# Last parts of experts in quarter blocks: 35 blocks instead of 36, with another order of the first batch's groups

## The chip, the cores and the metric

The kernel runs on one core of one Trainium2 chip. The metric is the device time of one execution in microseconds (us); the median of three runs before the change is 202.54 us (202.13 to 202.78). TensorE multiplies matrices; a weight load (the stationary operand) comes ahead of each matmul and is shown as an engine row of its own, PEld. VectorE (DVE), ScalarE (ACT) and GpSimd (POOL) work elementwise, and SyncE (SP) issues most of the DMA transfers.

## The reference, cut to what matters

Attention with a polynomial sketch feeds a mixture of experts that sends every token to one expert. All of it is in float32.

```python
# q, k, v: (4, 4, 1088, 32); S1, S2: (8, 32)
phi = lambda x: outer(S1 @ x, S2 @ x).reshape(64)        # per row
kv, z = sum_s phi(k) v^T, sum_s phi(k)
x = (phi(q) @ kv) / (phi(q) . z + 1e-6)                  # to (4352, 128)
logits = normalize(x) @ normalize(expert_emb).T / tau    # 8 experts
expert_idx = argmax(logits); gate_w = softmax(logits)[expert_idx]
for e in range(8):
    mask = expert_idx == e
    out[mask] = gate_w[mask, None] * (relu(x[mask] @ w1[e]) @ w2[e])   # F = 1024
```

With the inputs of the reference the eight experts get 524, 552, 568, 587, 623, 527, 504 and 467 of the 4352 tokens.

## The kernel before, in words

The four batches are handled as two pairs (m = 0 and 1). A pair has 17 tiles of 128 rows, in groups of four tiles and a rest of one (`GROUPS`). For a group of the first pair the steps are: turn the keys (`ktr0`, four transposes into a PSUM tile of tag `t`, then a copy by ScalarE), turn the queries (`qtr0`), the key sketch (`kab0`: 8 matmuls into the one PSUM bank `ab`), a copy of its second factor (`kb0`, ScalarE), the key products (`kp0`, VectorE, which reads the bank `ab` and that copy), the query sketch with its repeats (`pairs`: 16 matmuls into both PSUM tiles of tag `big`), two copies out of it (`sec`, ScalarE), two products (`prod`, VectorE), and the sum of keys by values (`kv0`: 16 matmuls for a group of four tiles). A float32 matmul shows as two records in the profile, one for each of its passes.

The program is emitted in an order written out by hand, and every engine keeps it. `HEAD` (L367) is the order of the first pair's steps and `ORDER` (L373) that of what follows; later work is put at a tick and a rank by `put_at`. Each tick is one block of tokens from tick `FIRST` on.

The tokens are grouped by expert into blocks of 128 rows, which are fetched with indirect DMAs (`fetch`), turned (`turn`, L936), multiplied by the first layer (`up`, L974), passed through ReLU (L992), multiplied by the second layer (`down`, L1014) and scattered to the output (L1032). `N` is 4352, and `FULL` is 30 blocks that certainly belong to one expert. The first ten (`EARLY`) are planned from the first pair alone, in `plan_early`; the other ones in `plan_late` (steps `count`, `rest`, `shared`, `others`, `experts`), whose numbers come out of the counts by small VectorE operations, and `table`, which finds the tokens of each block.

What an expert has left over beside whole blocks of 128 goes in halves of 64: the four blocks 30 to 33 (`SHARED`) take two experts, 64 rows each. In such a block (`two(i)`) each of the eight column groups of `up` is four matmuls of 64 stationary columns and 64 moving rows: two experts by two halves of the columns. `down` does two matmuls of 64 stationary columns for each of the eight parts of the sum, one per expert, into the two halves of the output's partitions:

```python
            for b, w in enumerate(ws):
                nc.tensor.matmul(ps[b * HALF:(b + 1) * HALF], h[:, f * P + b * HALF:f * P + (b + 1) * HALF], w[:, f],
                                 start=f == 0, stop=f == NF - 1, skip_group_check=True)
```

The second expert's first layer is loaded to its own place by SP (`weights_b`), and its second layer copied there by ScalarE (`second_weights_b`, L971). The straight line of the program has `USUAL` = 36 blocks. Behind it stands a conditional part for blocks 36 and 37 (`NBLK` = 38), which runs when the number of late blocks, read from memory by each engine (L1139), is above `USUAL - EARLY`.

Of the kernel before, what the change touches and what calls it, by code (L numbers as in the profile page):

```python
# [11 lines left out]
F32 = mybir.dt.float32  # L12
# [21 lines left out]
NBLK = ((N + E * (HALF - 1)) // HALF + 1) // 2  # L34
# [17 lines left out]
LATE = NBLK - EARLY  # L52
SHARED = E // 2
PAIRS = FULL - EARLY
AHEAD = 4
USUAL = N // P + 2
# [9 lines left out]
def kernel(  # L66
# [131 lines left out]
    def word(name):  # L198
        return consts.tile([2 * R, D], U32, name=name)
    top, rem, w, fits = word("s_top"), word("s_rem"), word("s_w"), word("s_fits")  # L200
# [10 lines left out]
    srow = consts.tile([2 * R, D], F32, name="srow")  # L211
# [3 lines left out]
    srows = consts.tile([2 * R, H, D], F32, name="srows")  # L215
# [30 lines left out]
    before, ones = consts.tile([P, P], BF16, name="before"), consts.tile([P, P], BF16, name="ones")  # L246
    less, more = consts.tile([P, E], BF16, name="less"), consts.tile([P, E], BF16, name="more")
    near = consts.tile([P, E], BF16, name="near")
    down_half = consts.tile([HALF, P], BF16, name="down_half")
    base = consts.tile([P, E], BF16, name="base")  # L250
# [9 lines left out]

    nowhere = [consts.tile([P, 2, n], BF16, name=f"nowhere{n}") for n in (EARLY, LATE + SHARED)]

    def more_constants():
        nc.vector.memset(ones, 1.0 / P)
        nc.vector.memset(ones_e, 1.0)

        nc.vector.memset(less, -(P - 1) / (2.0 * P))
        nc.vector.memset(more, (P - 1) / (2.0 * P))

        nc.vector.memset(near, -1.0 / (2.0 * P))  # L270
        nc.vector.memset(c_early, 0.0)
        nc.vector.memset(w_late, float(KEYS * E))
        for t in (place_k, place_r):
            nc.vector.memset(t, -1.0)
        for t, n in zip(nowhere, (EARLY, LATE)):
            nc.vector.memset(t, 0.0)
            nc.vector.memset(t[:, 0, :n], float(NOWHERE))

    def iotas():
# [5 lines left out]
        nc.vector.tensor_scalar(down_half, lane[:HALF], part[:HALF, 0:1], float(HALF), op0=ALU.subtract, op1=ALU.is_equal)  # L285
        nc.vector.tensor_scalar_mul(lanes, bview(lane, [[1, P], [0, WIDE]]), 1.0 / P)
# [69 lines left out]
prod 0 1; kab0 1; kb0 1; pairs 1; kp0 1; sec 1 0; sec 1 1; ktr0 2; qtr0 2; prod 1 0; prod 1 1; kab0 2; kb0 2; pairs 2;  # L356
kp0 2; sec 2 0; sec 2 1; ktr0 3; qtr0 3; prod 2 0; prod 2 1; clear 0; kv0 0; kab0 3; kb0 3; pairs 3; kp0 3; sec 3 0;
sec 3 1; ktr0 r; qtr0 r; prod 3 0; prod 3 1; kv0 1; norm emb; kab0 r; kb0 r; qab0 r; qb0 r; kp0 r; qp0 r; scale emb;
iotas; clear 1; ktr 0; kv0 2; kv0 3; kv0 r
# [84 lines left out]
    def keys(m, c0, c1, tick=None):  # L444
        n = c1 - c0
# [21 lines left out]
        def kv():  # L467

            if c0 == 0:
                acc[m] = ps_one("acc")[:, :8 * D].rearrange("p (i a n) -> p i a n", i=2, a=2)  # L470
            for c in range(c0, c1):
                rest = c == NC - 1
                for i in range(2) if rest else (c // NK,):
                    for p in range(2):
                        for u in range(2):
                            h = 2 * p + u
                            vo = v_rest[m][i][:, h] if rest else v_sb[m][:, h, c]
                            to_ones = (H - h) * D if rest else ((H - h) * 2 * NK - c) * D
                            nc.tensor.matmul(  # L479
                                acc[m][u * HALF:(u + 1) * HALF, i, p], s["kp"][:, c - c0, h],  # L480
                                bass.AP(tensor=vo.tensor, offset=vo.offset,
                                        ap=[list(vo.ap[0]), [to_ones, 2], [1, D]]),
                                start=p == 0 and c == 0, stop=rest, skip_group_check=True)
# [33 lines left out]
        steps.update({f"ktr0 {g}": tr, f"kab0 {g}": ab, f"kb0 {g}": b, f"kp0 {g}": prod, f"kv0 {g}": kv})  # L517
        if c1 == NC:
            steps.update({"total0": total, "trkv0": tr_kv, "kvT0": kvT, "kve0": lambda: kve(0), "kz0": lambda: kve(1)})
# [222 lines left out]
    SIZES = (EARLY, LATE)  # L742
# [3 lines left out]
    exp_i = [consts.tile([1, n], I32, name=f"exp_i{i}") for i, n in enumerate((EARLY, LATE + SHARED))]  # L746

    def blocks(which, upto, weight, place):

        n = SIZES[which]  # L750
        le = work.tile([P, n, E], F32, tag="le", bufs=2, name=f"le{which}")
        at = consts.tile([P, n + which * SHARED], F32, name=f"at{which}")[:, :n]
# [22 lines left out]
    def table(which, m1, key):  # L775
# [3 lines left out]
        n, w = SIZES[which] + which * SHARED, m1 * NCP  # L779
# [5 lines left out]
        def find():  # L785
            shape = [P, 3 * w * n]
            both = consts.tile(shape, BF16, name="hits0") if which == 0 else work.tile(
                [P, NC * ROW * 2], BF16, tag="xg0", bufs=1, name="hits1")[:, :3 * w * n]
# [16 lines left out]
        def first_rows():  # L805
            s["b"] = consts.tile([HALF, 2, SHARED], BF16, name="halves")
            nc.vector.tensor_copy(s["b"], s["ps"].rearrange("p (d n) -> p d n", d=2)[:HALF, :, LATE:])

        def halves():

            ps = s["ps"].rearrange("p (d n) -> p d n", d=2)
            nc.tensor.matmul(ps[:, :, PAIRS:PAIRS + SHARED], down_half, s["b"], start=False, stop=True, skip_group_check=True)

# [6 lines left out]
    def tokens_by_expert(rounded, out, ps):  # L820

        for j, r in enumerate(rounded):
            for i, t in enumerate([r] + counts):
                nc.tensor.matmul(ps[:, j * E:(j + 1) * E], ones, t, start=i == 0, stop=i == len(counts))
        nc.vector.tensor_scalar(out, ps, WHOLE, -WHOLE, op0=ALU.add, op1=ALU.add)

    def plan_early():
# [3 lines left out]
        def count():  # L831
            tokens_by_expert((less,), full, spare[0][:, NC * E:(NC + 1) * E])
# [15 lines left out]
    def plan_late():  # L848
# [4 lines left out]
        full, all_ = both[:, :E], both[:, E:]  # L853
        odd, odds, rank, key = column("odd"), column("odds"), column("odd_rank"), column("odd_key")
# [3 lines left out]
        def count():  # L858
            tokens_by_expert((near, more), both, table_bank[0][:, 1, :2 * E])
# [15 lines left out]
        def shared():  # L875

            s["high"] = column("high", w=SHARED)
            nc.vector.tensor_sub(odd, all_, full)
            nc.vector.tensor_tensor_scan(out=odds[:], data0=ones_e[:], data1=odd[:], initial=0.0, op0=ALU.mult, op1=ALU.add)
            nc.vector.tensor_scalar(rank, odd, -(NO_KEY + 1), NO_KEY, op0=ALU.mult, op1=ALU.add)  # L880
            nc.vector.tensor_add(rank, rank, odds)

            nc.vector.tensor_scalar(pairs, odds[:, E - 1:], 0.5, 0.25, op0=ALU.mult, op1=ALU.add)
            nc.vector.tensor_scalar(pairs, pairs, WHOLE, -WHOLE, op0=ALU.add, op1=ALU.add)
            nc.vector.scalar_tensor_tensor(out=key, in0=full, scalar=-NO_KEY, in1=base, op0=ALU.add, op1=ALU.add)
            n = 2 * SHARED
            is_it = work.tile([P, n, E], F32, tag="emb", bufs=2, name="is_it")
            it = work.tile([P, n, E], F32, tag="emb", bufs=2, name="it")
            s["keys"] = column("odd_keys", w=n)
            nc.vector.tensor_tensor(out=is_it, in0=bview(rank, [[0, n], [1, E]]),  # L890
                                    in1=bview(lane, [[1, n], [0, E]]), op=ALU.is_equal)
            nc.vector.tensor_mul(it, is_it, bview(key, [[0, n], [1, E]]))
            nc.vector.reduce_sum(out=s["keys"][:], in_=it, axis=AX.X)

        def others():
# [5 lines left out]
            halves = s["keys"][:].rearrange("p (n u) -> p n u", u=2)  # L901
            late["second"] = column("second_keys", w=SHARED)[0:1]
            late["keys"] = whole
            nc.vector.tensor_scalar_add(whole[:, LATE:], halves[:, :, 1], NO_KEY)

            nc.vector.tensor_tensor(out=late["second"], in0=whole[0:1, LATE:], in1=last[0:1], op=ALU.min)
            nc.vector.scalar_tensor_tensor(out=last, in0=halves[:, :, 0], scalar=NO_KEY, in1=last, op0=ALU.add, op1=ALU.min)
            late["key"] = whole

        def experts():  # L910
# [5 lines left out]
            nc.vector.tensor_scalar_min(exp_i[1], f, float(E - 1))  # L916
            late["n"] = consts.tile([1, 1], I32, name="n_late")
            nc.vector.tensor_add(late["n"], pairs[0:1], upto[0:1, E - 1:])
        return count, rest, shared, others, experts
# [4 lines left out]
    def of(i):  # L924
        return (0, i) if i < EARLY else (1, i - EARLY)
# [32 lines left out]


# [16 lines left out]
    def up(i):  # L976
# [3 lines left out]
        for u in range(2):  # L980
            for j in range(4):
# [4 lines left out]
                for b, wh in enumerate((w, first_b(i))):  # L986
                    for c in range(2):
                        r = slice(c * HALF, (c + 1) * HALF)
                        nc.tensor.matmul(ps[r, u, j * P + b * HALF:j * P + (b + 1) * HALF],  # L989
                                         wh[:, f * P + c * HALF:f * P + (c + 1) * HALF], x[:, b * HALF:(b + 1) * HALF],  # L990
                                         start=True, stop=True)
# [22 lines left out]
    def down(i):  # L1014
# [3 lines left out]
        for f in range(NF):  # L1018
# [3 lines left out]
            for b, w in enumerate(ws):  # L1022
                nc.tensor.matmul(ps[b * HALF:(b + 1) * HALF], h[:, f * P + b * HALF:f * P + (b + 1) * HALF], w[:, f],  # L1023
                                 start=f == 0, stop=f == NF - 1, skip_group_check=True)
# [54 lines left out]
    count, rest, shared, others, experts = plan_late()  # L1079
# [7 lines left out]
    put(2, 75.5, experts)  # L1087
    put(3, 73.5, find)
# [50 lines left out]
    n_late = nc.values_load(late["n"][:, :], min_val=0, max_val=LATE,  # L1139
                            skip_runtime_bounds_check_because="a count of blocks, of which there are no more")  # L1140
    with tc.If(n_late > USUAL - EARLY):
        put = put_at(-1)
        for i in range(USUAL, NBLK):
            put(0, 0, lambda i=i: fetch(i))
            if i < USUAL + 2:
                put(0, 1, lambda i=i: weights(i))
        put(0, 2, lambda: turn(USUAL))
        in_ticks(USUAL, NBLK, 0)
# [31 lines left out]
```

## Time and profile before

| | |
|---|---|
| median of three runs | 202.54 us |
| profiled execution, its own time | 204.43 us |
| span of the profiled instructions | 202.6 us |
| PE busy | 192.7 us (95%) |
| PE weight loads busy | 182.7 us (90%) |
| ACT, POOL, DVE busy | 102.4, 107.0, 87.6 us |
| granted TensorE clock | full in every slice |
| share of PE in the chain that ended last | 90% |

The span is what the instructions cover; the profiled execution's own time is 1.8 us more. Matmuls are pipelined: a record's duration is the latency of one matmul, and the distance between the starts of two matmuls is what one costs in a stream. In the chain that ended last, a row gives the start, the time until the chain moves on, and the line.

### The profile page before, as it was taken

The numbers are of one execution on the slowest core, as the hardware profiler recorded it, in microseconds if no ns is written. First come the engines' busy times: TensorE is split into PE (matmuls) and PEld (weight loads), VectorE is DVE, ScalarE is ACT, GpSimd is POOL, SyncE is SP. The second block draws the span as 40 slices with busy tenths as digits, with TensorE's granted clock in tenths as the row PEclk, the third lists the DMA queues.
The fourth block names the chain that finished last, engine by engine and source line by source line (L and its number), as shares of the span: only waits on it lengthen the run. The fifth ranks groups of instructions, "written<-read, shape, count | busy, mean of one in ns | idle before, by whom it ended". The sixth has DMA issues, their size and how long they took to land.

```text
span 202.6 us, 6949 instructions
## 1 busy us (share of the span) xinstructions
PE 192.7 (95%) x2586; PEld 182.7 (90%) x2586; DVE 87.6 (43%) x378; ACT 102.4 (51%) x293; POOL 107.0 (53%) x137
## 2 busy tenths in 40 slices
PE   7889999999799999999999999999999999999991
PEld 7667888889689999999999999999999999988991
DVE  6677848888658488912222212222122122112200
ACT  2657451436464456434655546545555465766540
POOL 4000335303813767755878777677676776664043
PEclk9999999999999999999999999999999999999999
DMA  4998799987284886544466665657646784485000
GB/s 132 323 217 287 179 320 293 280 282 208 54 321 139 278 310 211 165 132 145 148 205 189 170 205 155 209 166 163 222 147 184 223 306 169 136 263 190 3 26 25
DMA packets 28162, 39.42 MB, mean 195 GB/s; under 512 B 5738, under 2 KB 21366, under 8 KB 28130
## 3 DMA queue, kind: packets, MB, share of 16 engines
q1 hardware_dynamic: 25776, 34.23, 55.9%
q0 software_dynamic: 2304, 4.74, 7.5%
q8 instruction: 22, 0.36, 0.7%
q14 instruction: 10, 0.08, 0.1%
q10 hardware_dynamic: 50, 0.01, 0.0%
HBM read 34.37 MB, written 4.73 MB: 193 GB/s over the span
## 4 chain that ended last, share of the span: by engine, by line
PE 90%; DVE 4%; ACT 2%; issue 1%; DMA 1%; POOL 0%; POOLq 0%; DVEq 0%
PE ps_big L984 28%; PE ps_ab L1020 14%; PE ps_acc L1020 13%; PE ps_big L613 5%; PE ps_acc L479 4%; PE ps_big L989 4%; PE ps_t L382 3%; PE ps_t L936 2%; PE ps_ab L401 2%; PE ps_big L561 2%; PE ps_acc L1023 2%; PE ps_ab L1023 2%; PE ps_t L802 2%; ACT qpT L570 1%; PE ps_ab L591 1%
## 5 line engine op out<-in xcount | busy, mean ns | idle before, releaser
L984 PE MATMUL ps_big<-xTb,wb 128*128 128x128 f32 x512 | 63.0, 276 | 1.6 <-ACT xTb L938 1.4
L984 PEld LDWEIGHTS ps_big<-xTb,wb 128*128 128x128 f32 x512 | 59.7, 192 | 2.4 <-ACT xTb L938 1.6
L1032 POOL DMA_INDIRECT out_dram<-y,dst_i x36 | 37.7, 1048 | 42.9 <-ACT y L1029 24.4
L992 ACT ACTIVATE hT<-ps_big 128x1024 f32<-128x1024 f32 x36 | 36.9, 1024 | 41.3 <-issue 22.7
L930 POOL DMA_INDIRECT xs<-rows,dst_i x36 | 37.3, 1035 | 18.8 <-DVE dst_i L817 11.3
L938 DVE COPY xTb<-ps_t 128x128 f32<-128x128 f32 x29 | 8.4, 290 | 59.4 <-issue 38.2
L1020 PE MATMUL ps_ab<-w_sb,hT 128*128 x256 | 31.3, 275 | 0.0
L1020 PE MATMUL ps_acc<-w_sb,hT 128*128 x256 | 31.2, 275 | 0.0
L1020 PEld LDWEIGHTS ps_ab<-w_sb,hT 128*128 128x128 f32 x256 | 29.9, 192 | 0.0
L1020 PEld LDWEIGHTS ps_acc<-w_sb,hT 128*128 128x128 f32 x256 | 29.9, 192 | 0.0
L998 POOL TENSOR_TENSOR norm<-norm,half_c 128x1 f32<-128x1 f32 x36 | 21.6, 604 | 4.5 <-ACT sq L997 4.1
L1011 DVE TENSOR_SCALAR gate<-gate 128x1 f32<-128x1 f32 x36 | 5.5, 152 | 23.2 <-ACT probs L1008 16.4
L1029 ACT ACTIVATE y<-ps_ab,gate 128x128 f32<-128x128 f32 x17 | 6.2, 367 | 11.0 <-PE ps_ab L1020 6.4
L1029 ACT ACTIVATE y<-ps_acc,gate 128x128 f32<-128x128 f32 x18 | 6.6, 366 | 9.9 <-PE ps_acc L1020 6.8
L1008 ACT ACTIVATE probs<-xs,norm 128x8 f32<-128x8 f32 x36 | 10.6, 295 | 1.2 <-DVE norm L1001 1.2
L997 ACT ACTIVATE sq<-xs 128x128 f32<-128x128 f32 x36 | 10.8, 301 | 0.2
L936 PE MATMUL ps_t<-ident,xs 128*128 128x128 f32 x36 | 10.2, 282 | 0.2 <-issue 0.2
L417 POOL TENSOR_TENSOR kp<-both 128x1024 f32<-128x1024 f32 (+1 forms) x4 | 6.5, 1624 | 7.0 <-ACT both L412 4.8
L479 PE MATMUL ps_acc<-v,kp 128*64 128x64 f32 x256 | 9.2, 225 | 0.5 <-issue 0.5
L319 POOL TENSOR_TENSOR emb_ss<-emb_ss,half_c 8x1 f32<-8x1 f32 x1 | 0.6, 576 | 17.1 <-ACT emb_sq L318 17.1
L479 PEld LDWEIGHTS ps_acc<-v,kp 128*64 128x64 f32 x256 | 8.2, 138 | 1.5 <-issue 1.5
L989 PE MATMUL ps_big<-xTb,wb 128*64 128x64 f32 x128 | 8.3, 224 | 0.3 <-issue 0.2
(254 smaller groups left out, 293.7 us busy)
## 6 DMA issues: line engine op xcount, KB each, us to landing
wb<-in_moe_w_dram SPq DMA_DIRECT2D x36, 512.0 KB
w_sb<-in_moe_w_dram SPq DMA_DIRECT2D x16, 256.0 KB
rows<-xg SPq DMA_DIRECT2D x4, 544.0 KB
v<-in_v_dram SPq DMA_DIRECT2D x4, 512.0 KB
v<-in_moe_w_dram SPq DMA_DIRECT2D x4, 512.0 KB
k<-in_k_dram SPq DMA_DIRECT2D x3, 512.0 KB
q<-in_q_dram SPq DMA_DIRECT2D x3, 512.0 KB
xs<-rows,dst_i POOLq DMA_INDIRECT x36
```

The lines of the kernel that those rows point to most:

```text
L479: nc.tensor.matmul(acc[m][u * HALF:(u + 1) * HALF, i, p], s["kp"][:, c - c0, h], bass.AP(tensor=vo.tensor, offset=vo.offset, ap=[list(vo.a ...
L930: nc.gpsimd.indirect_dma_start(out=xs[i][:], out_offset=None, in_=rows[:2 * S if t == 0 else N + 1], in_offset=bass.IndirectOffsetOnAxis(a ...
L936: nc.tensor.transpose(ps[:, :P], xs[i][:, :DM], ident)
L984: nc.tensor.matmul(ps[:, u, j * P:(j + 1) * P], w[:, f * P:(f + 1) * P], x, start=True, stop=True)
L989: nc.tensor.matmul(ps[r, u, j * P + b * HALF:j * P + (b + 1) * HALF], wh[:, f * P + c * HALF:f * P + (c + 1) * HALF], x[:, b * HALF:(b + 1 ...
L992: nc.scalar.activation(hT[i], ps, ACT.Relu)
L997: nc.scalar.activation(sq, xs[i][:, :DM], ACT.Square, accum_out=norms[i])
L998: nc.gpsimd.tensor_tensor(out=norms[i], in0=norms[i], in1=half_c, op=ALU.pow)
L1008: nc.scalar.activation(p, xs[i][:, DM:], ACT.Exp, scale=norms.pop(i)[:, 0:1], accum_out=gate[i])
L1020: nc.tensor.matmul(ps, h[:, f * P:(f + 1) * P], ws[0][:, f], start=f == 0, stop=f == NF - 1)
L1029: nc.scalar.activation(y, ps, ACT.Copy, scale=gate.pop(i)[:, 0:1])
L1032: d = nc.gpsimd.indirect_dma_start(out=out[:, :], out_offset=bass.IndirectOffsetOnAxis(ap=dst_i[t][:, j:j + 1], axis=0), in_=y[:], in_offs ...
```

## The change

The leftovers of experts are cut in quarters of 32 rows instead of halves. `near` and `more` get other constants, so that a leftover above 96 rows counts as a whole block and the rest is counted in quarters (`parts`, 1 to 3). Three blocks (30 to 32) take two experts each: 30 and 31 hold a quarter of one and three quarters of another (`MIXED`, `cut(i)` = 32), and 32 holds two halves. The experts are ranked by their number of quarters (`score`, `ahead`, `rank`), and `RANKS` says which rank goes where. What doesn't fit in these six places (`over`) sets off the conditional part, which now has nine blocks and builds a table of its own (`extra`). The straight line has 35 blocks.

In the two mixed blocks a matmul of `up` has 32 or 96 moving rows, and the order of the four matmuls alternates the halves of the columns. `down` does three matmuls per part of the sum there: 32, 32 and 64 stationary columns. In `HEAD` the step `pairs` of groups 1 to 3 stands ahead of `kab0`, `qtr0` ahead of `ktr0`, `kp0` behind the two `prod`, and `kv0 0` is cut in two halves, of which the second comes behind group 3. Nine small memsets and two small VectorE operations are added to the constants (`fours`, `order`, one more pair of `nowhere`; `down_quart`, `last_first`), `halves` of the table becomes two matmuls, and some early tiles move to the pool `work`. In the diff below parts are left out.

```diff
-LATE = NBLK - EARLY
-SHARED = E // 2
+USUAL = N // P + 1
+LATE = USUAL - EARLY
+QUART = P // 4
+SHARED = 3
+MIXED = 2
+RANKS = (4, 5, 2, 0, 1, 3)
+SPILL = 3
+EXTRA = SPILL + E - 2
...
-USUAL = N // P + 2
...
     def more_constants():
         nc.vector.memset(ones, 1.0 / P)
+        nc.vector.memset(fours, 4.0 / P)
...
-        nc.vector.memset(more, (P - 1) / (2.0 * P))
-
-        nc.vector.memset(near, -1.0 / (2.0 * P))
+        nc.vector.memset(more, (QUART - 1) / (2.0 * P))
+
+        nc.vector.memset(near, -(HALF + 1) / (2.0 * P))
+        for i, rank in enumerate(RANKS):
+            nc.vector.memset(order[:, i:i + 1], float(rank))
...
-prod 0 1; kab0 1; kb0 1; pairs 1; kp0 1; sec 1 0; sec 1 1; ktr0 2; qtr0 2; prod 1 0; prod 1 1; kab0 2; kb0 2; pairs 2;
-kp0 2; sec 2 0; sec 2 1; ktr0 3; qtr0 3; prod 2 0; prod 2 1; clear 0; kv0 0; kab0 3; kb0 3; pairs 3; kp0 3; sec 3 0;
-sec 3 1; ktr0 r; qtr0 r; prod 3 0; prod 3 1; kv0 1; norm emb; kab0 r; kb0 r; qab0 r; qb0 r; kp0 r; qp0 r; scale emb;
-iotas; clear 1; ktr 0; kv0 2; kv0 3; kv0 r
+prod 0 1; pairs 1; kab0 1; sec 1 0; sec 1 1; qtr0 2; kb0 1; ktr0 2; prod 1 0; prod 1 1; kp0 1; pairs 2; kab0 2;
+sec 2 0; sec 2 1; qtr0 3; kb0 2; ktr0 3; prod 2 0; prod 2 1; kp0 2; clear 0; kv0 first; pairs 3; kab0 3; sec 3 0;
+sec 3 1; kb0 3; ktr0 r; qtr0 r; prod 3 0; prod 3 1; kp0 3; kv0 second; kv0 1; norm emb; kab0 r; kb0 r; qab0 r; qb0 r;
+kp0 r; qp0 r; scale emb; iotas; clear 1; ktr 0; kv0 2; kv0 3; kv0 r
...
+            nc.vector.scalar_tensor_tensor(out=parts, in0=full, scalar=-4.0, in1=quarters, op0=ALU.mult, op1=ALU.add)
+            nc.vector.tensor_scalar_min(odd, parts, 1.0)
+            score = column("score")
+            nc.vector.scalar_tensor_tensor(out=score, in0=parts, scalar=float(E), in1=last_first, op0=ALU.mult, op1=ALU.add)
...
+    def cut(i):
+        return QUART if i < FULL + MIXED else HALF
...
-                for b, wh in enumerate((w, first_b(i))):
-                    for c in range(2):
-                        r = slice(c * HALF, (c + 1) * HALF)
-                        nc.tensor.matmul(ps[r, u, j * P + b * HALF:j * P + (b + 1) * HALF],
-                                         wh[:, f * P + c * HALF:f * P + (c + 1) * HALF], x[:, b * HALF:(b + 1) * HALF],
-                                         start=True, stop=True)
+                for b, c in ((0, 0), (1, 1), (0, 1), (1, 0)):
+                    r = slice(c * HALF, (c + 1) * HALF)
+                    n0, n1 = ((0, cut(i)), (cut(i), P))[b]
+                    nc.tensor.matmul(ps[r, u, j * P + n0:j * P + n1],
+                                     (w, first_b(i))[b][:, f * P + c * HALF:f * P + (c + 1) * HALF], x[:, n0:n1],
+                                     start=True, stop=True)
...
-            for b, w in enumerate(ws):
-                nc.tensor.matmul(ps[b * HALF:(b + 1) * HALF], h[:, f * P + b * HALF:f * P + (b + 1) * HALF], w[:, f],
-                                 start=f == 0, stop=f == NF - 1, skip_group_check=True)
+            for n0, n1 in ((0, cut(i)), (cut(i), HALF), (HALF, P)):
+                if n0 < n1:
+                    nc.tensor.matmul(ps[n0:n1], h[:, f * P + n0:f * P + n1], ws[int(n0 > 0)][:, f],
+                                     start=f == 0, stop=f == NF - 1, skip_group_check=True)
...
-        for i in range(USUAL, NBLK):
-            put(0, 0, lambda i=i: fetch(i))
+        find, high, low, sums, tokens, *_ = table(2, NM, lambda: late["extra_key"])
+        for f in (extra, find, high, low, sums, lambda: tokens(0, EXTRA)):
+            put_at(-1)(0, -1, f)
+        for i in range(USUAL, USUAL + EXTRA):
+            put_at(max(i - USUAL - AHEAD, -1))(0, 0, lambda i=i: fetch(i))
```

## The prediction

> **What bounds the kernel now.** I read the page first: busy shares, then the chain of work that ended last.
>
> ```profile
> PE 192.7 (95%) x2586; PEld 182.7 (90%) x2586; DVE 87.6 (43%) x378; ACT 102.4 (51%) x293; POOL 107.0 (53%) x137
> ...
> PE 90%; DVE 4%; ACT 2%; issue 1%; DMA 1%; POOL 0%; POOLq 0%; DVEq 0%
> ```
>
> TensorE is the chain for 90% of the span, so a change counts by the PE time that it takes or gives, and by PE's waits in the first 24 us. Next I cut the chain to the shared blocks:
>
> ```profile
> 169.59 0.11 PE ps_t L936
> 169.70 1.79 PE ps_acc L1020 x16
> ...
> 182.93 1.90 PE ps_ab L1023 x32
> 184.83 1.86 PE ps_big L989 x64
> 186.69 0.26 PE ps_t L936
> 186.96 1.90 PE ps_acc L1023 x32
> 188.85 1.98 PE ps_big L984 x16
> ```
>
> An ordinary block is 1.79 (up) + 0.11 (turn) + 1.79 (down) = 3.69 us. The last shared block, from 184.66 to 188.78, is 4.12; the three before it are 4.54, 4.47 and 4.25, two of them with a pause of "issue" inside. The turn takes 0.26 here, not 0.11, though it is the same instruction. The timeline of PE shows why:
>
> ```profile
> 186.41 0.29 PE L989 MATMUL ps_big<-xTb,v 128*64 128x64 f32 x4
> 186.63 0.33 PE L936 MATMUL ps_t<-ident,xs 128*128 128x128 f32 x1
> 186.88 0.32 PE L1023 MATMUL ps_acc<-w_sb,hT 128*64 x1
> 186.89 0.32 PE L1023 MATMUL ps_acc<-v,hT 128*64 128x128 f32 x1
> ```
>
> The four L989 matmuls start in two pairs, at 186.41 and 186.47. A stream of them would go on at 186.53; the turn's weight load begins at 186.62, some 0.1 us later, and its load no longer hides behind the matmul ahead. The pairs of L1023 themselves start together (186.88 and 186.89): matmuls on the two column halves run side by side. From pair to pair it is 0.11 us (1.90 for 16 pairs, the first with its load exposed). Lastly I took one line's durations:
>
> ```profile
> L989 PEld LDWEIGHTS ps_big<-xTb,wb x128: 132/138/139, 171.4 to 186.3; 128*64 128x64 f32 x128
> ```
>
> A load of 64 columns shows 138 ns, one of 128 columns 192 (page, L984): 54 ns for 64 columns, the rest is latency.
>
> **What the skill says.** "TensorEngine Tiling (Array Packing)", section Tiling Modes: "Changing tiling mode (not just tile) drains the TensorE"; 128x64 and 128x32 are listed as two configurations. The trace agrees for the changes it has (128 to 64 columns and back, above; 64-column to 32-row tiles, L401 to L561, also 0.1 us). It has no switch between 64 and 32 columns. "TensorE: Matmul & The Clock Gate", section LDWEIGHTS: a load costs its columns by 1/1.2 GHz, so 53 ns for 64 and 27 for 32; the 54 above agrees. The same page, Part 3 (Packing small matmuls), describes masks of 32-column strips and three 32-column tiles at 2.38x; that speaks for the first rival.
>
> **Does it take 35 blocks?** From the counts of the reference's inputs: whole blocks with the cut above 96 are 4, 4, 4, 4, 5, 4, 4, 3 = 32, leftovers 12, 40, 56, 75, 0, 15, 0, 83, so quarters 1, 2, 2, 3, 0, 1, 0, 3. Two threes with two ones, two twos together: all six places fit. 32 + 3 = 35; late blocks 35 - 10 = 25, not above 25. The conditional part stays out; the nearest edge is 8 tokens away (56 against 64).
>
> **The parts, one by one.**
>
> (a) One shared block less: its up, turn, down, and with them on other queues two 512 KB loads and three POOL steps, all hidden behind PE. I take 4.2 us, between 4.12 and 4.25, the two without a pause. **-4.2** (-4.1 to -4.5).
>
> (b) `down` of the two mixed blocks. Now 8 parts by two concurrent matmuls of two passes: 2 x 0.11 = 0.22 us per part. After: 32, 32 and 64 columns. If 32 and 64 are two modes, a part is: the two 32s side by side, 2 x 0.11; a switch, 0.10 drain + 0.05 load of 64 columns that nothing hides; the 64 alone, 2 x 0.11; a switch back, 0.10 + 0.03. Sum 0.44 + 0.28 = 0.72, so 0.50 more per part, 4.0 per block, less 0.13 as the last switch back is no extra: 3.85. Two blocks: **+7.7**. From below: the three strips run side by side without drain, 0. From above I see nothing that makes it more than a drain of 0.15 at each switch, +9.2. I take 7.7, since every change of tile size in this trace drains.
>
> (c) `up` of the mixed blocks. Now 0.058 per pair of passes (four records each 0.117), four pairs: 0.233 per column group. After, per column half: two passes with 32 rows (27 ns of rows) and two with 96 (80 ns). The load of the next weights takes 53 ns and hides only behind the pass ahead, so the short ones cost 53: 2 x 58 + 2 x 85 = 286 ns with the 5 ns of overhead seen. +0.053 x 8 = 0.43 per block, **+0.9** for two. If a short one always waits for the long one beside it, 4 x 85 = 340: +1.7. If loads hide fully, 0. Block 32 has 64 by 64 in alternating halves, as before: 0.
>
> (d) `HEAD`. The group's loop before, from the chain: sketch 9.61, `pairs` 10.23, `sec` 11.42, key copy 12.38, next sketch 13.04, a period of 3.43. I followed both orders by hand with the trace's durations (sketch 0.62 to the next, pairs 1.05, `sec` 0.48 apart, copy 0.60, `prod` 0.61 apart, `kp0` 1.15, 0.1 us for each mode switch); the old order comes out with `pairs` at 10.23, 13.65, 17.39 (trace: 10.23, 13.65, 17.28). The new order gives 10.09, 13.25, 16.83: the loop now is pairs, `sec`, two `prod`. That is 0.56 gained by group 3. But what the old order had done before it stands behind it now: sketch 3 (0.62) and half of `kv0 0` (0.5). And there is a new wait: the sketches share the one bank `ab`, which `kp0` of the group ahead reads, and `kp0` is queued on DVE behind two `prod` that wait for `sec`. Sketch 2 waits until 14.52 for `kp0 1`, sketch 3 until 17.89 for `kp0 2`; behind them in PE's queue are the turns of the next group. The first sketch of the rest group comes at 20.38 instead of 19.88, and PE then runs without slack to 32.97 in the chain. **+0.5** (-0.4 if `kp0` is never awaited, +0.8).
>
> (e) Nine memsets at the start: twelve took 0.58 (1.50 to 2.08), so nine are 0.45, and DVE stood idle for 0.37 before the sketch words landed. That DVE chain is what starts the kernel: **+0.1** (0 to 0.45). `down_quart` and `last_first` (0.49 + 0.15, by the row of `down_half`) delay `en_blk` to about 26.7 with (d); its reader on PE comes at 26.55 + 0.5: hidden by 0.3; without that cover up to +0.4.
>
> (f) The plan of the late blocks: some five more DVE operations of 0.15 to 0.25, about 1 us at 73 to 78 us. The three passes over `hits` (1.36 each) shrink by an eighth, 0.5 in all. DVE ends the last at 85.9 and PE takes up the sums at 87.84: hidden by 1.9. Late next would be the fetches of blocks 10 and 11. One matmul more in `halves`: 0.06. `number` is three tiny operations at a tick where DVE waits. 0.
>
> (g) At the end the compare and branch (0.37 on PE, hidden by the last down) is the same; the code behind is longer but not run. 0.
>
> Sum: -4.2 + 7.7 + 0.9 + 0.5 + 0.1 = +5.0. The profiled execution's own time is 204.43 (span 202.6), so it would be 209.4; the median of the runs lies 1.9 below that, 202.54, and 202.54 + 5.0 = **207.5 us**.
>
> **The rivals.**
>
> First, no drain between strips. If what counts is whether the strips overlap, 0 to 31, 32 to 63 and 64 to 127 never do: (b) falls to 0. For it: every switch in this trace is between tiles that overlap, and the pairs of L1023 and L561 show that disjoint tiles run freely. Against it: the skill's sentence. Then -4.2 + 0.9 + 0.5 + 0.1 = -2.7: 199.8, from 198.8 to 201.4. This ends on the other side. The point that decides: the saving pays for -2.7 / 16 parts, so below 0.17 us more per part the change is faster, above it slower.
>
> Second, no drain, but the 64 doesn't run beside the 32s: a part is 0.44, +3.5 for two blocks, +0.8 in all: 203.3, from 202 to 204.5.
>
> Third, the conditional part runs after all: nine blocks of at least 3.69 and a table, about +36: 240. The counts speak against it.
>
> **How the numbers follow.** Drain 0.57, free strips 0.34, serial 0.08, conditional 0.01. A difference within 0.3% (0.6 us) can't be told from none in this kernel. Free strips are faster throughout; of serial half is the same; the rest is slower: faster 0.34, same 0.04, slower 0.62. The likeliest alone ranges from 205.3 (up hides, head gains) to 208.6; with the free strips the range is 198.8 to 208.6.
>
> **What would show it.** (b): the three `down` groups of a mixed block at some 5.8 us instead of 1.9, with steps of 0.25 us between 32- and 64-column matmuls; if free, all three start together every 0.11. (c): the 0.233 per column group at 0.29. (d): `pairs` near 10.1, 13.25, 16.8 and the sketch between them waiting for DVE; the first turn of the second pair at 21.3 instead of 20.65. (a): 35 scatters. I am wrong if 32 and 64 columns share a mode, if the hardware sorts matmuls by tile over more than one part, or if the instruction pauses seen in blocks 30 and 31 grow with the new stream.

## The result, and the profile after

| | before | after |
|---|---|---|
| median of six runs | 202.24 us (202.01 to 202.78) | 209.38 us (208.43 to 210.3) |
| profiled execution, its own time | 204.43 us | 208.94 us |
| span | 202.6 us | 207.2 us |
| ratio to before | 1 | 1.0336, 95% interval 1.0303 to 1.0369 |

The change costs 7.1 us where 5.0 were predicted; 209.38 lies 0.8 us above the upper end of the range.

The page of the kernel after, its busy shares and the first line of its chain:

```profile
PE 196.6 (95%) x2522; PEld 181.9 (88%) x2522; DVE 87.9 (42%) x391; ACT 99.4 (48%) x286; POOL 104.7 (51%) x134
...
PE 92%; DVE 3%; ACT 2%; issue 1%; POOL 0%; POOLq 0%
```

TensorE has 64 matmul records less than before and is busy 3.9 us longer; it is still nine tenths of the chain. Most of the loss is therefore to be looked for in how long its matmuls take. The chain through the shared blocks shows which (start, time until the chain moves on, engine and line; rows between the ones named are left out in this and the later chains):

```profile
171.51 2.38 PE ps_big L1044 x44
175.95 2.40 PE ps_big L1044 x45
178.61 5.49 PE ps_acc L1079 x47
184.25 1.86 PE ps_big L1044 x62
186.37 5.64 PE ps_ab L1079 x48
192.01 1.98 PE ps_big L1039 x16
194.10 1.90 PE ps_acc L1079 x32
196.00 1.98 PE ps_big L1039 x16
```

The second layer (L1079) takes 5.64 us in each of blocks 30 and 31 (178.61 to 184.25, of which the chain has 5.49 in one piece, and 186.37 to 192.01), and 1.90 in block 32, whose two halves are as they were before. The first layer (L1044) takes 2.38 and 2.40 us in the mixed blocks and 1.86 in block 32. From the first shared block to the second ordinary block behind them (171.51 to 196.00) it is 24.49 us. Before, it was 171.49 to 192.84, 21.35 us, with one block more:

```profile
171.49 1.83 PE ps_big L989 x57
...
192.84 1.98 PE ps_big L984 x16
```

Only 3.1 us of the 7.1 are here by these two traces. But the trace of before has pauses in that stretch which other traces of the same code don't have (experiment 7), and a pause of 1.40 us ahead of its first block, which make the loss look smaller. From the first block's first layer to the first shared block it is 116.2 us before (55.26 to 171.49) and 116.2 after (55.35 to 171.51), so the long middle costs nothing. The other losses are at the two ends of the kernel, and the experiments part them.

One part of a mixed block's second layer, TensorE's weight loads in the timeline of after (start, busy time, tiles, shape; the bracket is idle time before the row):

```profile
178.54 0.11 PEld L1079 LDWEIGHTS ps_acc<-w_sb,hT 128*32 128x32 f32 x1
178.54 0.11 PEld L1079 LDWEIGHTS ps_acc<-v,hT 128*32 128x32 f32 x1
178.56 0.11 PEld L1079 LDWEIGHTS ps_acc<-w_sb,hT 128*32 128x32 f32 x1
178.57 0.11 PEld L1079 LDWEIGHTS ps_acc<-v,hT 128*32 128x32 f32 x1
178.88 0.19 PEld L1079 LDWEIGHTS ps_acc<-v,hT 128*64 128x64 f32 x2 [0.20 <-issue]
179.24 0.11 PEld L1079 LDWEIGHTS ps_acc<-w_sb,hT 128*32 128x32 f32 x1 [0.17 <-issue]
```

The four loads of 32 columns (two experts, two passes) come within 0.03 us of each other. The load of 64 columns waits 0.20 us with nothing in the profile to wait for, and the next 32 waits 0.17. From part to part it is 178.54 to 179.24, 0.70 us, against 0.22 for a part before. The prediction said 0.72.

### The profile page after: what moved, and what is told of

Its sections match the earlier page's. It is cut to its first block, busy times and chain, and to the rows that moved or that the text cites. A ratio compares the mean times of both kernels' runs of the same rounds, so it can differ in the third digit from the quotient of the medians.

```text
span 207.2 us, 6806 instructions
## 1 busy us (share of the span) xinstructions
PE 196.6 (95%) x2522; PEld 181.9 (88%) x2522; DVE 87.9 (42%) x391; ACT 99.4 (48%) x286; POOL 104.7 (51%) x134
## 4 chain that ended last, share of the span: by engine, by line
PE 92%; DVE 3%; ACT 2%; issue 1%; POOL 0%; POOLq 0%
PE ps_big L1039 27%; PE ps_ab L1075 14%; PE ps_acc L1075 13%; PE ps_big L627 5%; PE ps_acc L491 5%; PE ps_acc L1079 4%; PE ps_t L394 4%; PE ps_big L1044 3%; PE ps_ab L1079 3%; PE ps_t L988 2%; PE ps_ab L413 2%; PE ps_big L575 2%; PE ps_t L817 1%; PE ps_acc L109 1%; PE ps_big L605 1%
## 5 line engine op out<-in xcount | busy, mean ns | idle before, releaser
L1047 ACT ACTIVATE hT<-ps_big 128x1024 f32<-128x1024 f32 x35 | 35.8, 1024 | 40.2 <-PE ps_big L1039 38.7
L982 POOL DMA_INDIRECT xs<-rows,dst_i x35 | 36.1, 1031 | 18.7 <-DVE dst_i L834 11.3
L1053 POOL TENSOR_TENSOR norm<-norm,half_c 128x1 f32<-128x1 f32 x35 | 20.8, 598 | 2.8 <-ACT sq L1052 2.5
L491 PE MATMUL ps_acc<-v,kp 128*64 128x64 f32 x256 | 9.2, 225 | 1.2 <-issue 1.2
L491 PEld LDWEIGHTS ps_acc<-v,kp 128*64 128x64 f32 x256 | 8.2, 138 | 2.2 <-issue 2.2
L396 ACT COPY qT<-ps_t 128x512 f32<-128x512 f32 (+1 forms) x10 | 5.2, 530 | 5.6 <-PE ps_t L394 4.8
```

What stands on the lines that cost most here:

```text
L491: nc.tensor.matmul(acc[m][u * HALF:(u + 1) * HALF, i, p], s["kp"][:, c - at0, h], bass.AP(tensor=vo.tensor, offset=vo.offset, ap=[list(vo. ...
L982: nc.gpsimd.indirect_dma_start(out=xs[i][:], out_offset=None, in_=rows[:2 * S if t == 0 else N + 1], in_offset=bass.IndirectOffsetOnAxis(a ...
L1047: nc.scalar.activation(hT[i], ps, ACT.Relu)
L1053: nc.gpsimd.tensor_tensor(out=norms[i], in0=norms[i], in1=half_c, op=ALU.pow)
```

## The experiments

Each ratio is to the kernel before on the same chip, with its 95% interval. Experiments 1 to 4 ran on one chip, 5 to 8 on a second, 9 to 11 on a third. On the third the kernel before itself took 205.55 us, so there the traces are compared, and ratios with reserve.

**1. The second layer in four strips of 32 columns.** The three quarters become three strips, so that no tile size changes inside a block.

```diff
-            for n0, n1 in ((0, cut(i)), (cut(i), HALF), (HALF, P)):
+            q = QUART if cut(i) < HALF else HALF
+            for n0 in range(0, P, q):
+                n1 = n0 + q
                 if n0 < n1:
-                    nc.tensor.matmul(ps[n0:n1], h[:, f * P + n0:f * P + n1], ws[int(n0 > 0)][:, f],
+                    nc.tensor.matmul(ps[n0:n1], h[:, f * P + n0:f * P + n1], ws[int(n0 >= cut(i))][:, f],
```

> The changed kernel with the down of blocks 30 and 31 in four strips of 32 columns (0-31, 32-63, 64-95, 96-127) instead of 32, 32 and 64, so that all of a block's down has one tile mode; nothing else is changed. Theory 1 (each change between 32 and 64 columns drains): a part of the sum falls from 0.71 to 0.22 us, 16 parts, 7.8 us less than the changed kernel: about 201.6 us, level with the kernel before. Theory 2 (no drain, the matmuls of different strips simply take turns): four turns of 0.22 instead of three, a part at 0.88: about 212 us.

Measured: 202.58 us (22 runs), ratio 0.9991 (0.9967 to 1.0015). The chain of this run at the two second layers:

```profile
178.07 1.89 PE ps_acc L1081 x64
182.50 1.89 PE ps_ab L1081 x64
```

More matmuls (64 records instead of 48), and a third of the time: 1.89 us instead of 5.64 in each of the two blocks, 7.5 us in both. The four strips of a part run side by side. So the mixture of 32 and 64 columns in the second layer is the loss of this stage; experiment 2 parts it further. That the shared stage is now 170.97 to 188.38, 17.41 us against 24.49, says the same: 7.1 us.

**2. All 32s of a block first, then its 64s.** The same matmuls, with one change of tile size inside a block's second layer instead of fifteen.

```diff
+        def part(f, n0, n1):
+            nc.tensor.matmul(ps[n0:n1], h[:, f * P + n0:f * P + n1], ws[int(n0 > 0)][:, f],
+                             start=f == 0, stop=f == NF - 1, skip_group_check=True)
+        mixed = two(i) and cut(i) < HALF
...
-            for n0, n1 in ((0, cut(i)), (cut(i), HALF), (HALF, P)):
...
+            for n0, n1 in ((0, cut(i)), (cut(i), HALF)) if mixed else ((0, HALF), (HALF, P)):
+                part(f, n0, n1)
+        for f in range(NF if mixed else 0):
+            part(f, HALF, P)
```

> The changed kernel with the same 32, 32 and 64 columns in blocks 30 and 31, but sorted: first the two 32s of all eight parts, then the eight 64s. The matmuls are the same ones, the changes of tile size fall from 15 to 1 inside a block. Theory 1 (drains): 14 changes of some 0.13 less per block, 3.7 us in all for two blocks: about 205.7 us, and down of a block at 3.8 us instead of 5.5. Theory 2 (turns without drains): no difference, 209.4 us.

Measured: 205.42 us, ratio 1.0123 (1.009 to 1.0157). The chain:

```profile
179.20 3.44 PE ps_acc L1074 x45
182.96 1.86 PE ps_big L1044 x62
185.08 3.76 PE ps_ab L1074 x48
```

A block takes 3.76 us here (179.20 to 182.96, and 3.76 in the last row). Two sweeps of eight parts at 0.22 us would be 3.5 us, and one switch is left. Against the 5.64 of the changed kernel, 14 switches less save 1.88 us per block, 0.13 us per switch. So two effects add up: the switches, and that the 64s, which have a sweep of their own here, don't share the time of the 32s (1.89 us for all of it in strips). How much of a switch is a drain, and how much the weight load behind it that nothing hides, these runs don't separate.

**3. The changed kernel with the order of before at the start.**

```diff
-prod 0 1; pairs 1; kab0 1; sec 1 0; sec 1 1; qtr0 2; kb0 1; ktr0 2; prod 1 0; prod 1 1; kp0 1; pairs 2; kab0 2;
+prod 0 1; kab0 1; kb0 1; pairs 1; kp0 1; sec 1 0; sec 1 1; ktr0 2; qtr0 2; prod 1 0; prod 1 1; kab0 2; kb0 2; pairs 2;
...
```

> The changed kernel with the order HEAD of the kernel before (and so no split of kv0 0). If the new order costs the 0.5 us of the prediction: about 208.9 us. Rival, that the new order is what the prediction missed (the first steps of the second pair are 2.4 us later in the profile of the changed kernel): about 207.0 us.

Measured: 207.95 us, ratio 1.0238 (1.02 to 1.0275), against 1.0336 with the new order: 1.4 us less by the medians, 2.0 by the ratios (0.0098 of 202.5).

**4. The kernel before with the new order at the start.** The reverse edit, with `kv0 0` cut in two as the change does.

```diff
-prod 0 1; kab0 1; kb0 1; pairs 1; kp0 1; sec 1 0; sec 1 1; ktr0 2; qtr0 2; prod 1 0; prod 1 1; kab0 2; kb0 2; pairs 2;
+prod 0 1; pairs 1; kab0 1; sec 1 0; sec 1 1; qtr0 2; kb0 1; ktr0 2; prod 1 0; prod 1 1; kp0 1; pairs 2; kab0 2;
...
```

> The kernel before with the new order HEAD alone, kv0 0 in two halves. With the 0.5 us of the prediction: about 202.7 us. Rival, that the order costs the 2.4 us by which the second pair starts later in the profile of the changed kernel: about 204.6 us.

Measured: 203.81 us, ratio 1.0056 (1.003 to 1.0082), +1.1 us (0.6 to 1.7). The new order costs more than the 0.5 predicted, in either kernel. The timeline of TensorE in the changed kernel, from the first turn of group 1 to the first turn of the second pair (L394), where `pairs` is L575, the key sketch L413 and the first pair's sum over keys L491:

```profile
8.07 0.66 PE L394 MATMUL ps_t<-ident,k 128*128 128x128 f32 x4
...
13.32 1.26 PE L575 MATMUL ps_big<-qT,S_pairs 32*64 32x256 f32 x32 [0.24 <-ACT qT L396]
14.84 0.69 PE L413 MATMUL ps_ab<-Sblk,kT 128*64 128x64 f32 x16 [0.26 <-DVE kp L429]
...
17.09 1.12 PE L575 MATMUL ps_big<-qT,S_pairs 32*64 32x256 f32 x32
18.31 0.69 PE L413 MATMUL ps_ab<-Sblk,kT 128*64 128x64 f32 x16
...
19.29 1.62 PE L491 MATMUL ps_acc<-v,kp 128*64 128x64 f32 x48
...
21.58 0.66 PE L394 MATMUL ps_t<-ident,k 128*128 128x128 f32 x4
```

and the same stretch before (turns L382, `pairs` L561, sketch L401, sum L479):

```profile
7.86 0.66 PE L382 MATMUL ps_t<-ident,k 128*128 128x128 f32 x4
...
16.71 0.64 PE L401 MATMUL ps_ab<-Sblk,kT 128*64 128x64 f32 x16
17.28 1.12 PE L561 MATMUL ps_big<-qT,S_pairs 32*64 32x256 f32 x32
...
18.69 1.15 PE L479 MATMUL ps_acc<-v,kp 128*64 128x64 f32 x32
...
20.65 0.66 PE L382 MATMUL ps_t<-ident,k 128*128 128x128 f32 x4
```

The new order brings the last `pairs` forward by 0.19 us only (17.28 to 17.09). Behind it stand a sketch at 18.31 that had been done at 16.71, and 48 records of the sum instead of 32. The first turn of the second pair starts at 21.58 instead of 20.65. Of these 0.93 us the new order makes 0.72: up to the first turn of group 1 both orders are alike, and from there it is 13.51 us (8.07 to 21.58) instead of 12.79 (7.86 to 20.65). The other traces of this order have 13.50 or 13.51 (experiments 1, 2 and 11), those of the old one 12.79 (3, 5, 6 and 8); in experiments 4 and 7 a load of `q` came 0.6 to 0.7 us late in this stretch.

**5. Strips and the old order together.** Both edits, 1 and 3.

> The changed kernel with both edits of the first runs: the second product of the mixed blocks in four strips of 32 columns, and the old order of the groups at the start. The tail theory says that three terms are independent: 202.58 (strips alone) less the 1.4 that the old order gave to the changed kernel, or the 1.1 that the new order cost the kernel before, gives 201.2 to 201.5 us, ratio 0.993 to 0.995 to the kernel before. Of that, the tail after the last matmul stays at 5.9 us. If the loss at the start only hides another wait that shows now, it stays at 202.3 to 202.8.

Measured: 200.93 us, ratio 0.991 (0.9879 to 0.9941). The terms add up, and this complete kernel is faster than both: 1.8 us (1.2 to 2.5) faster than before. It keeps 35 blocks without their price. By the ratios the old order takes 1.6 us off the strips of experiment 1 (0.0081 of 203).

**6. As 5, with two blocks behind the jump instead of nine.** By now a third loss had shown. From the start of the last matmul to the end of the span it was 4.52 us before (198.12 to 202.65), and 4.53 in experiment 4; it was 5.89 in the changed kernel (201.28 to 207.17), and 5.90, 5.92 and 6.00 in experiments 1 to 3. All kernels with the longer conditional part have it.

```diff
-        for i in range(USUAL, USUAL + EXTRA):
+        for i in range(USUAL, USUAL + 2):
...
-        in_ticks(USUAL, USUAL + EXTRA, 0)
+        in_ticks(USUAL, USUAL + 2, 0)
```

> As the strips with the old order, but the conditional part behind holds two blocks instead of nine (its table stays). With these inputs it doesn't run either way; other inputs would lose tokens. Theory of the long jump: the stretch from the last matmul to the end is 5.9 us because TensorE's compare-and-branch lasts 3.3 to 3.8 us instead of 0.37 and GpSimd's first instructions behind the jump have to be fetched; with two blocks to jump over it falls to 4.5 to 5.0, and the time by 0.9 to 1.4 us, to 199.9 to 200.5. Rival: the longer end comes from the last block or from the semaphores, not from the jump: 5.9 stays, and the time is that of the strips with the old order, 201.3.

Measured: 200.32 us, ratio 0.9898 (0.9853 to 0.9943); by the times alone it can't be told from 5. In the trace the last stretch is 4.76 us (193.89 to 198.65) against 6.02 in experiment 5 (193.27 to 199.29). The instructions of the conditional's line in the changed kernel (engine's sequencer, operation, count, shortest, median and longest duration in ns, first and last start):

```profile
L1198 POOLq EVENT_SEMAPHORE  x5: 17/43/43, 203.0 to 205.2; - x5
L1198 PEldq COMPARE_BRANCH  x1: 3679/3679/3679, 200.5 to 200.5; - x1
L1198 POOLq COMPARE_BRANCH  x1: 50/50/50, 202.6 to 202.6; - x1
```

and in experiment 6:

```profile
L1200 POOLq EVENT_SEMAPHORE  x3: 17/17/43, 195.4 to 195.5; - x3
...
L1200 PEldq COMPARE_BRANCH  x1: 370/370/370, 193.1 to 193.1; - x1
```

The branch is taken in both. With nine blocks to jump over it lasts 3.68 us on TensorE, with two 0.37. GpSimd's branch lasts 0.05 us either way, but its first instructions at the place jumped to spread over 2.2 us (203.0 to 205.2, five of 17 to 43 ns); in experiment 6 it is three in 0.2 us. The end follows GpSimd's delay rather than TensorE's branch. In the nine traces with a long part to jump over, the step that comes late is 2.50 to 2.69 us behind GpSimd's own branch, whether TensorE's branch lasted 3.3 us or 3.8; it is 0.5 to 1.2 us behind TensorE's last step. The traffic of the DMA queues from the last matmul on has a possible reason, here after and then experiment 6 (packets, MB, share of the engines):

```profile
q8 instruction: 2, 0.03, 2.2%
q14 instruction: 2, 0.02, 1.1%
```

```profile
q8 instruction: 1, 0.02, 1.2%
```

Four fetches of instructions instead of one, and a fifth just before the last matmul. That GpSimd waits for such fetches is not shown: no wait of that kind is recorded, and only the times suggest it (201.22 and 201.48, as TensorE's branch hangs; 203.50, 203.66 and 204.87, between GpSimd's steps). The last one lands at 205.78, when GpSimd had gone on at 205.06.

**7. The kernel before with its two conditional blocks four times in a row**, eight to jump over.

```diff
-        put = put_at(-1)
-        for i in range(USUAL, NBLK):
...
+        for _ in range(4):
+            put = put_at(-1)
+            for i in range(USUAL, NBLK):
...
```

> The kernel before, whose conditional part of two blocks stands four times in a row: eight blocks that don't run with these inputs. Theory of the long jump: TensorE's branch goes from 0.37 to over 3 us and the stretch from the last matmul to the end from 4.5 to about 5.8 us, the time from 202.4 to 203.6, ratio 1.005 to 1.007. Rival (the end is longer for another reason): nothing changes, 202.4, ratio 1.000.

Measured: 203.67 us (16 runs) beside 203.0, ratio 1.0047 (1.0017 to 1.0076), +1.0 us (0.3 to 1.5). The last stretch is 5.75 us (196.82 to 202.57) instead of 4.52:

```profile
L1141 PEldq COMPARE_BRANCH  x1: 3319/3319/3319, 196.0 to 196.0; - x1
```

So the length of what is jumped over makes the loss: +1.2 us when it is added to before, -1.3 when taken from experiment 5. This trace also shows what the shared blocks of before take without the pauses:

```profile
171.19 2.02 PE ps_big L989 x64
175.25 2.02 PE ps_big L989 x64
...
191.54 1.98 PE ps_big L984 x16
```

171.19 to 191.54 is 20.35 us for the stretch that took 21.35 in the profile of before and 24.49 after: the stage costs 4.1 us, not 3.1.

**8. The first layer of the mixed blocks in the order of before**, so that equal widths stand beside each other; otherwise as 5.

```diff
-                for b, c in ((0, 0), (1, 1), (0, 1), (1, 0)):
+                for b, c in ((0, 0), (0, 1), (1, 0), (1, 1)):
```

> As the strips with the old order, but the four products of a mixed block's first layer in the order of the kernel before: both column halves of the 32 tokens, then both of the 96, so that equal ones stand beside each other; the changed kernel has a 32 beside a 96. If a short product waits for the long one beside it (0.298 us per column group measured, 0.286 predicted for independent halves, 0.340 for full waiting), equal neighbours bring it to 0.28 or less: 2.25 us per block instead of 2.38, 0.2 to 0.3 us in all, 201.0. If the halves are independent, nothing changes, 201.3. If the same half twice in a row was what hid the loads, it is 0.3 per column group or more and up to 0.5 us worse.

Measured: 201.69 us, ratio 0.9942 (0.9912 to 0.9972), not told apart from 5. The chain:

```profile
169.44 2.40 PE ps_big L1044 x64
173.89 2.40 PE ps_big L1044 x64
```

2.40 us in either order: which widths stand side by side doesn't matter, as the prediction's working had it (each column half for itself). A wait of the short one for the long one is excluded.

**9. The key copy and product ahead of the group's products.** With the strips; TensorE's new order is kept, and only ScalarE's and VectorE's queues change. It tests whether the sketch's wait for `kp0` is the loss of experiment 4.

```diff
-prod 0 1; pairs 1; kab0 1; sec 1 0; sec 1 1; qtr0 2; kb0 1; ktr0 2; prod 1 0; prod 1 1; kp0 1; pairs 2; kab0 2;
-sec 2 0; sec 2 1; qtr0 3; kb0 2; ktr0 3; prod 2 0; prod 2 1; kp0 2; clear 0; ...
+prod 0 1; pairs 1; kab0 1; kb0 1; kp0 1; sec 1 0; sec 1 1; qtr0 2; ktr0 2; prod 1 0; prod 1 1; pairs 2; kab0 2;
+kb0 2; kp0 2; sec 2 0; sec 2 1; qtr0 3; ktr0 3; prod 2 0; prod 2 1; clear 0; ...
```

> The strips with the new order on TensorE kept as it is, but in the first batch's groups 1 and 2 the copy kb and the key product kp stand ahead of the group's two copies qpT on ScalarE and its two products on VectorE. Theory that the loss at the start is the key sketch's wait for kp, as it is queued on VectorE behind two products: the sketches of groups 2 and 3 (14.84 and 18.31 in the changed kernel, behind pairs at 13.32 and 17.09) go at most 0.7 us behind their pairs, the first turn of the second pair comes back to 20.9 or less from 21.58, and the time is 201.0 to 201.8 us, ratio 0.992 to 0.995 (the strips alone 0.999, with the old order 0.991). Rival: the pairs were never the bound and the later copies and products are, so that what kp gains the two products lose: the turn stays at 21.4 to 21.8, and the time is that of the strips, 0.997 to 1.001.

Measured: 206.7 us beside 205.55, ratio 1.0038 (1.0012 to 1.0063), where the strips alone have 0.9991. My theory falls. TensorE's and VectorE's timelines:

```profile
14.30 1.71 PE L575 MATMUL ps_big<-qT,S_pairs 32*64 32x256 f32 x32 [1.29 <-ACT kT L396]
15.94 0.69 PE L413 MATMUL ps_ab<-Sblk,kT 128*64 128x64 f32 x16
...
12.33 1.23 DVE L429 TENSOR_TENSOR kp<-ps_ab,kb 128x1024 f32<-128x1024 f32 x1 [2.28 <-ACT kb L419]
13.47 1.28 DVE L587 TENSOR_TENSOR held<-ps_big,qpT 128x512 f32<-128x512 f32 x2
```

The sketch has no idle time before it any more, yet the second of these `pairs` comes 4.05 us behind the first (10.25 to 14.30), where it is 3.00 in the changed kernel (10.32 to 13.32) and in experiment 11, and the first turn of the second pair comes at 23.84. On this chip the changed kernel's own order has that turn at 21.91 (experiment 11). Two queues are held up. On ScalarE `kb`, which waits for the sketch until 12.04, now stands ahead of the group's copies; the profile names the last of them, of turned keys (13.63 to 14.26), as what ended the wait of `pairs`. On VectorE the products, which empty the banks that the next `pairs` fills, stand behind the 1.23 us of `kp`: they start at 13.47, where the changed kernel starts them at 12.13, and the first ends at 14.15. The two ends lie 0.1 us apart, so this run doesn't tell which of them sets the pace. The 0.26 us of waiting for `kp` are the cheap side of that exchange.

**10. The old order with `pairs` ahead of the sketch, and nothing else moved**, with the strips.

```diff
-prod 0 1; kab0 1; kb0 1; pairs 1; kp0 1; sec 1 0; sec 1 1; ktr0 2; qtr0 2; prod 1 0; prod 1 1; kab0 2; kb0 2; pairs 2;
+prod 0 1; pairs 1; kab0 1; kb0 1; kp0 1; sec 1 0; sec 1 1; ktr0 2; qtr0 2; prod 1 0; prod 1 1; pairs 2; kab0 2; kb0 2;
...
```

> The strips with the order of the groups before, except that each group's eight products stand ahead of its key sketch; turns, copies, the key product and the undivided first sum over keys are where they were. Theory of the wait for kp: without it the swap costs nothing by itself, the turn of the second pair comes at 20.7 to 21.0 and the ratio is 0.991 to 0.994, as with the old order. Rival: what costs is the swap itself (the sketch behind the pairs makes the key copy, and with it the products, late): turn at 21.3 or later, ratio 0.996 to 0.999.

Measured: 205.9 us, ratio 1.0016 (0.9986 to 1.0046); the turn of the second pair at 24.11. The rival is right that the swap by itself costs (it had the turn at 21.3 or later): with `kb` and `kp` in front of the copies and products, the sketch behind `pairs` makes both late, as in 9. Here `pairs` starts at 14.77, just behind ScalarE's copy of the turned queries that it reads (14.09 to 14.71). With `kab0` ahead, the old order had this copy and product under way before `pairs` ended.

**11. The changed kernel with two blocks behind the jump, nothing else.** The edit of 6 alone.

> The changed kernel with two of the nine blocks in the conditional part, nothing else undone; it doesn't run with these inputs, other inputs would lose tokens. Theory of the long jump: the stretch from the last matmul to the end goes from 5.9 to 4.6 to 4.8 us, the branch on TensorE from 3.7 to 0.37, the time from 209.4 to about 208.2, ratio 1.027 to 1.030 instead of 1.034. Rival (the jump is hidden in unprofiled runs): 1.034.

Measured: 209.72 us beside 205.55, ratio 1.0212 (1.0174 to 1.0251). The last stretch is 4.75 us (203.25 to 208.00) instead of 5.89, and the branch 0.37, as expected. The ratio lies below the 1.027 to 1.030 expected and fell by twice what these 1.1 us explain. The kernel before is some 3 us slower on this chip than on the others, and the changed kernel itself was not run here, so the ratio is no measure of the jump.

## Why the prediction was right or wrong

The direction, the mechanism of the shared blocks and the largest term were right. The sum was 2.1 us short, because one term that was put at nothing, the end of the kernel, cost 1.2 us, and another, the order at the start, was mis-sized.

| step | predicted | shown |
|---|---|---|
| (a) to (c), the shared stage | +4.4 | +4.1 (24.49 - 20.35) |
| of it (b), the mixed second layers | +7.7 | +7.5 in the chain, 7.0 by the ratios (1.0336 - 0.9991; experiment 1) |
| of it (c), `up` | +0.9 | +0.7 (2.38 and 2.40 against 2.02) |
| (d), the order at the start | +0.5 | +1.1 (experiment 4), 1.4 to 2.0 (experiment 3), 1.6 (1 and 5); 0.72 of it placed in the traces |
| (g), the end | 0 | +1.2 (experiment 7), 1.3 (experiment 6), 1.1 (experiment 11) |
| sum with (e), (f) | +5.0 | +7.1 measured |

**(b)** held. It rested on one pause of 0.1 us between other tile sizes and on the sentence of the Trainium skill, "TensorEngine Tiling (Array Packing)", section Tiling Modes, that a change of tiling mode drains TensorE. The trace agrees that a change between 32 and 64 columns costs time, 0.13 us each. Of the 7.5 us some 3.7 are that the two sizes don't run side by side (3.76 against 1.89 in experiments 2 and 1) and 3.8 are the switches; the prediction's working had 3.5 and 4.2. The first rival (free strips) was excluded by the loads at 178.88 and 179.24, the second (no drain, only no overlap, 3.5 us a block) by experiment 2, which makes nearly that kernel and takes 3.76 us a block instead of 5.64. The third rival did not happen: 35 blocks ran.

**(c)** was close, from a base that was too low: it used 0.233 us per column group where the two blocks show 2.02 / 8 = 0.25 without pauses, and 0.286 where 2.38 / 8 = 0.30 came.

**(d)** is the smaller failed term. The times put it at 1.1 to 2.0 us, above the 0.5. Its working by hand held better than that: from 20.65 before to 21.3 it saw 0.65 us until the first turn of the second pair, and the traces have 0.72 (12.79 to 13.51), as `pairs` gains and the sketch and half of the sum stand behind it. Only 0.5 was then put into the sum. The turn came at 21.58 and not at 21.3 because the first turn of group 1 was already 0.21 us late (8.07 instead of 7.86), ahead of anything that the new order changes. What the new order costs in the times beyond 0.72 us is not placed.

**(g)** is the larger failed term, and it was put at nothing: "the code behind is longer but not run. 0." The code isn't run, but it is jumped over. The profile of before had the branch at 0.37 us, hidden by the last second layer, and I carried that number over to a jump of nine blocks without giving it another bound. With nine blocks it is 3.68 us, GpSimd's steps behind its own jump spread over 2.2 us, and the end comes 1.1 to 1.3 us later. The range had no share for it, and its upper end of 208.6 lay below the result; with 1.2 more it would not have.

Stage, start and end make 4.1 + 1.1 to 2.0 + 1.1 to 1.3, 6.3 to 7.4 us, with the measured 7.1 between. Of (f), the plan of the late blocks, nothing is seen: it lies in the middle stretch, which takes 116.2 us in both. The memsets, (e), were not measured by themselves: the first turn of group 1 starts at 7.80 to 7.87 in the three traces without them (before, 4 and 7) and at 7.60 to 8.49 in those with them.

**The pauses** that the prediction's last sentence warned of did not grow in the changed kernel: the ones in blocks 30 and 31 are gone in after. Three others remain open. In the first layer of block 32 there is one of 0.88, 1.14 and 1.79 us in experiments 5, 6 and 9, which have the strips; experiments 1, 8 and 10 have the strips too, and at most 0.06. A pause of 1.36 to 1.42 us of TensorE ahead of the first block's first layer is in the profiles of before and of experiments 9 to 11, and in no other. One inside the first pair's sum over keys is in the profile of after, and shorter in those of experiments 2 (0.92) and 11 (0.37). Experiments 1 and 4 have the same order there without it, but they pause for 0.47 and 0.58 us in the second pair's sum, 10 us later, as before does for 0.49:

```profile
24.03 1.67 PE L491 MATMUL ps_acc<-v,kp 128*64 128x64 f32 x49 [1.19 <-issue]
```

Such a pause can be part of what the new order costs in the times beyond 0.72 us; that wasn't tested.

## What to carry to other kernels

Where pieces of different size share a stream of matmuls, try to cut the larger one into strips of the smaller size, even if that makes more instructions (here 64 records in 1.89 us against 48 in 5.6). Code that never runs isn't free if every execution jumps over it at its very end; look at the branch and at what each engine does after it. And in a ring of engines, what the next round waits for goes ahead of what only a later one needs: experiment 9 saved a wait of 0.26 us and lost 1.93 us by late copies and products (the turn at 23.84 against 21.91).

## What the runs showed of the hardware that was not expected

- A taken branch over eight or nine blocks of instructions lasted 3.3 to 3.8 us on TensorE, over two blocks 0.37. The end of the kernel came 1.1 to 1.3 us later. GpSimd's five instructions behind its own jump spread over 2.2 us in after (three in 0.2 us before), and the late one of them kept to 2.50 to 2.69 us behind GpSimd's branch in all nine traces.
- Four matmuls of 32 stationary columns, with moving operands of two experts, run side by side at full overlap: eight parts with four strips in 1.89 us, as long as two halves of 64 take (1.90).
- A switch between 32 and 64 columns cost 0.13 us (14 switches less saved 1.88 us per block), and the two sizes never ran side by side: sorted by size, a block takes 3.76 us instead of 1.89.
- The same kernel took 202.2 to 203.0 us on some chips and 205.6 on another.
